# All of h by twenty block products for twenty-four, from the fifth unit on, in trees over six banks

## The chip, the cores and the metric

The kernel runs on one core of a Trainium2 chip, in f32 throughout. The metric is the device time of one execution in microseconds (us). The engines are PE (matmuls, with the weight loads PEld beside them), DVE, ACT, POOL, and SP, which issues most DMAs. Each engine runs its own queue of instructions in order; semaphores tie the queues together.

## The reference

```python
B, H, S, D = 4, 8, 768, 48
f = 1.0 / (1.0 + np.exp(-f_logit))
for t in range(S):
    state = f[:, :, t, :, None] * state + einsum('bhd,bhe->bhde', k[:, :, t], v[:, :, t])
    y[:, :, t] = einsum('bhd,bhde->bhe', q[:, :, t], state)
x = y.transpose(0, 2, 1, 3).reshape(3072, 384)
h = x @ w_in                                  # 384 x 2048
out = (h * (1.0 / (1.0 + np.exp(-1.702 * h)))) @ w_out     # 2048 x 384
```

A recurrence with a decay per channel (the attention part) makes x; a perceptron with the quick gelu follows.

## The kernel before, in words

**Units.** The 3072 tokens are cut into 12 units of 256 (4 batches of 3). Each has an attention part and a perceptron part. The attention of unit n + 1 is interleaved with the perceptron of unit n and earlier ones: `merge` (L1100) walks the attention's parts of a unit, and behind each takes as many items from a list `fill` of perceptron matmuls as its share of the columns says (`late`, L1141, gives the shares from unit 4 on; L1146 and the loop at L1178 the columns of a unit). PE's and POOL's queues hold the instructions in the order in which the program emits them; the queues of DVE and ACT are put in order by the tile framework's scheduler from unit 4's attention on (`fill_order.close()`).

**Attention.** Inputs come by DMA and are turned by DVE transpositions (`turn`, L338). In six levels, PE makes scores into the tile "sc" (two PSUM banks, one buffer: `score` L406), DVE and ACT evacuate them (`evacuate` L435, L445, L456), DVE multiplies the operands by products of the gates (`promote` L492), ACT sets copies aside (L463, L469), and v is shuffled on DVE (L304). POOL makes the products of the gates (L397, L365). In units 4 to 10, DVE turns k (L558), a DMA brings it to DRAM and back, and ACT copies it (`fetch_k`, L573). Then the part "S" (or "S1"): `add` (L503) begins the outputs in the tile "y" (two banks); PE makes the state increments into "sc" (L594); DVE updates the states (L612, L613); and the part "W" adds the states' share into "y" (L634), ACT copies it out (L646), DMAs bring it into xT, and POOL makes sums of its blocks (`sums_of_x`, eleven sums of 128 x 128, L856).

**Perceptron.** Units 0 to 2 run in blocks of four column tiles (`mlp_h` L980, `mlp_o` L994) while the weights are converted. Unit 3 makes h plainly (L980). From unit 3 on, the second matmul runs by seven products for eight (`mlp_o7`, L785), with sums of g on DVE (`sums_of_a`, L720 to L724, and `last_sum`, L729) and sums of w_out (T).

From unit 4 on ("the fifth unit on"), h is made by `mlp_h16` (L873): the first three quarters of the 2048 columns by sixteen block products for eighteen, the last quarter plainly. With w_in as blocks of 128 x 512 and xT as blocks of 128 x 128, `CHAINS` (L796) lists four chains of products `(weights, tokens, output)`, all of a chain accumulating in one bank; `SEQUENCE` (L804) gives the order and `LANE` (L805) the bank of each of four (tags mm0 to mm3). A product is four matmuls of 128 columns (L883). After some products of a chain, the bank's present sum is a share of an output block of h: ACT copies the first share into g (L897), DVE adds the second (L899) and ACT takes the gelu (L900); one output needs a gelu alone (L894). The last quarter's matmuls (L905, 256 columns, gelu L909) lie between. The last unit has one token more, so its products are of 129 columns and run in two groups of two matmuls.

The sums of weight blocks come from `sums_of_w` (L810: eleven sums, nine on POOL, L816, and two on DVE, L820), three behind each part of unit 4's attention as `chores`, and from `sums_in_place` (L829: seven sums that overwrite w_in, L840, L842), which unit 3's list holds behind its first eight matmuls of o (L1027), when plain h has been read for the last time.

Of the kernel before, what the change touches and what calls it, by code (L numbers as in the profile page):

```python
# [23 lines left out]
def kernel(  # L24
# [706 lines left out]
    def mlp_o7(n, g):  # L731
# [37 lines left out]
        def p3():  # L769
# [6 lines left out]
            ("Y", a(0, 0), b(0, 0), p1, True, 0), ("W", a(1, 1), T_(4), p4, True, 1),  # L776
# [18 lines left out]
    ROWS = NFF // FG - 1  # L795
    CHAINS = (  # L796
        (("D5", "b21", 3), ("N6", "E12", 2), ("C4", "E4", 4), ("N3", "E15", 0), ("a00", "E6", 1), ("N4", "E10", 5)),
        (("N5", "b21", None), ("N1", "b11", 1), ("D11", "E11", None), ("D8", "E3", 0)),
        (("a22", "E3", None), ("D9", "E9", 4), ("N7", "b10", None), ("N2", "E14", 2)),
        (("a10", "E0", None), ("D2", "b11", 3)),  # L800
    )
    NEGATIVE = 0, 2, 5

    SEQUENCE = "0 1 2 0 1 2 p 0 1 2 p 0 1 2 p 0 3 3 p 0".split()  # L804
    LANE = {"0": 0, "1": 1, "2": 2, "3": 1, "p": 3}  # L805
    lanes = {}
    WA = {f"a{i}{c}": w_in[:, c, i * FG * P:(i + 1) * FG * P] for i in range(ROWS) for c in range(NK)}
    assert ROWS == 3 and NK == 3

    def sums_of_w():  # L810

        for i in range(1, 8):
            WA[f"N{i}"] = const.tile([P, FG * P], F32, name=f"N{i}")

        def by(engine, op):
            return lambda out, x, y: lambda: engine.tensor_tensor(WA[out], WA[x], WA[y], op)  # L816
        plus, minus = by(nc.gpsimd, ALU.add), by(nc.gpsimd, ALU.subtract)

        def both_minus(out, x, y):
            return lambda: nc.vector.scalar_tensor_tensor(  # L820
                WA[out], WA[x], -1.0, WA[y], op0=ALU.mult, op1=ALU.subtract
            )
        yield from (
            both_minus("N4", "a00", "a20"), both_minus("N7", "a10", "a11"), plus("N6", "a20", "a21"),
            minus("N7", "N7", "N6"), plus("N2", "a12", "a22"), minus("N6", "N6", "N2"), plus("N6", "N6", "a10"),
            minus("N3", "a00", "a21"), plus("N1", "a01", "a21"), plus("N5", "a02", "a22"), plus("N5", "N5", "N4"),
        )

    def sums_in_place():  # L829

        assert not w_sums
        for new, old in (("D5", "a12"), ("D2", "a11"), ("D9", "a21"), ("C4", "a20"), ("D11", "a01"), ("D8", "a02")):
            WA[new] = WA[old]
        add, sub = ALU.add, ALU.subtract
        for engine, out, x, op, y in (
            (nc.gpsimd, "D5", "a12", sub, "a10"), (nc.vector, "D9", "a20", add, "a21"),
            (nc.vector, "C4", "a22", sub, "a20"), (nc.vector, "C4", "C4", add, "D5"),
            (nc.gpsimd, "D2", "a10", add, "a11"),
        ):
            engine.tensor_tensor(WA[out], WA[x], WA[y], op)  # L840
        for out, x, y in (("D11", "a01", "a00"), ("D8", "D11", "a02")):
            nc.vector.scalar_tensor_tensor(WA[out], WA[x], -1.0, WA[y], op0=ALU.mult, op1=ALU.subtract)  # L842

    def sums_of_x(n):
# [6 lines left out]

        def by(out, x, op, y):
            e.setdefault(out, None)
            if e[out] is None:
                e[out] = next(at)
            nc.gpsimd.tensor_tensor(e[out], e[x], e[y], op)  # L856

        add, sub = ALU.add, ALU.subtract
        by("E4", "b10", sub, "b00")
        by("E12", "E4", add, "b21")  # L860
        by("E3", "b20", add, "b21")
        by("E10", "b01", add, "b21")
        by("E0", "E10", sub, "b11")
        by("E15", "E12", add, "b11")
        by("E6", "E10", sub, "E15")
        by("E9", "b00", sub, "b21")
        by("E11", "b10", add, "b11")
        by("E11", "E11", add, "E3")
        by("E14", "E4", sub, "b20")

    E = {}

    def mlp_h16(n, g):  # L873
        w = (width(n) + 1) // 2
        banks, begun = {}, set()

        def product(group, chain, i, lane):
            a, b, out = CHAINS[chain][i]
            if i == 0:
                banks[chain] = bank([P, group.stop - group.start, w], f"h_{n}_{group.start}_{chain}", lane)  # L880
            ph = banks[chain]
            for t in range(group.start, group.stop):
                nc.tensor.matmul(  # L883
                    ph[:, t - group.start], lhsT=WA[a][:, t * P:(t + 1) * P], rhs=E[n][b],
                    start=(i == 0 and t == group.start), stop=(i == len(CHAINS[chain]) - 1), skip_group_check=True,
                )
            if out is None:
                return
            row, j = out // 2, out % 2
            f = row * FG + group.start  # L890
# [11 lines left out]
        def plain(f, lane):  # L902
            ph = bank([P, width(n)], f"h_{n}_p{f}", lane)
            for c in range(NK):
                nc.tensor.matmul(  # L905
                    ph, lhsT=w_in[:, c, (ROWS * FG + f) * P:(ROWS * FG + f + 1) * P], rhs=xTs[n][:, c, :], start=(c == 0),
                    stop=(c == NK - 1),
                )
# [302 lines left out]
```

## Time and profile before

| what | before |
|---|---|
| median of 3 runs (lowest, highest) | 616.76 us (615.52, 617.32) |
| profiled execution, its own time | 615.66 us |
| its span | 613.9 us |
| DVE, ACT, POOL busy | 66%, 44%, 20% |
| PE groups on the chain that ended last | h L883 19%, h L980 13%, h_p L905 7%, o_Y, o_Z, o_X and o_W L785 28% together |
| L492 on DVE (promote) | 45 of them, 1295 ns each |
| L899 on DVE (add of h) | 45, 627 ns |
| L897 and L900 on ACT (copy, gelu) | 45 each, 541 and 585 ns |
| L338 on DVE (transposition) | 36, 1108 ns |

The busy table says how much of the span each engine worked. The chain that ended last follows the end of the kernel back, at each step to what released it, and gives shares by engine and line. A timeline's row has the start, the duration, the engine, the line, the operation, what it writes and reads, and in brackets how long the engine stood still before it and what released it. Rows of PE group several matmuls, and neighbouring groups overlap, because matmuls are pipelined: what one costs PE is the distance of the starts.

### The profile page before, as it was taken

Reading aid. Unit: us, or ns where it says so; the run is one execution under the profiler, and the core shown is the slowest. Engines: PE = TensorE matmul, PEld = TensorE weight load, DVE = VectorE, ACT = ScalarE, POOL = GpSimd, SP = SyncE. Lnnn points to the kernel's source line nnn. Section 1 sums busy time; section 2 is a strip of 40 time slices with the busy share of each in tenths; the row PEclk is TensorE's granted clock in tenths of the full one; section 3 lists DMA queues with packets and bytes.
Section 4 is the critical chain, followed back from the end, with each engine's and each line's share of the span. In section 5 each row is a group of like instructions: output and inputs, shape, how many; then the busy total and the mean of one; then the engine's idle time right before and its main releaser. Section 6 shows DMA issues by size and latency. Waiting matters only on the chain.

```text
span 613.9 us, 18222 instructions
## 1 busy us (share of the span) xinstructions
PE 593.2 (97%) x7760; PEld 526.7 (86%) x7760; DVE 405.4 (66%) x649; ACT 271.5 (44%) x580; POOL 121.5 (20%) x201
## 2 busy tenths in 40 slices
PE   7969899969999999999999999999999999999997
PEld 5657676847677689999999999999999999999997
DVE  1788966665885856777667578667679565442254
ACT  3475633433333444454464364264364363343330
POOL 3020120020003802501401501501401402301100
PEclk9889999989999999999999999999999999999999
DMA  7756766553034453443453343453261121001000
GB/s 174 196 125 179 182 150 173 130 144 79 1 95 101 106 137 90 96 121 92 113 138 71 79 104 84 126 136 75 61 163 40 40 60 28 28 2 28 27 0 27
DMA packets 83313, 58.28 MB, mean 95 GB/s; under 512 B 33633, under 2 KB 75265, under 8 KB 83233
## 3 DMA queue, kind: packets, MB, share of 16 engines
q1 hardware_dynamic: 82480, 55.94, 36.6%
q10 hardware_dynamic: 753, 1.18, 0.8%
q8 instruction: 61, 1.00, 0.7%
q14 instruction: 19, 0.16, 0.1%
HBM read 43.98 MB, written 8.39 MB: 85 GB/s over the span
## 4 chain that ended last, share of the span: by engine, by line
PE 90%; DVE 5%; ACT 1%; DMA 1%; issue 1%; SPq 1%; DVEq 0%; ACTq 0%
PE h L883 19%; PE h L980 13%; PE o_Y L785 12%; PE o L994 9%; PE o_Z L785 8%; PE h_p L905 7%; PE sc L406 6%; PE o_X L785 4%; PE o_W L785 4%; PE t L350 2%; PE y L634 2%; PE y L503 2%; PE sc L594 2%; PE idle L114 1%; DVE a L227 1%
## 5 line engine op out<-in xcount | busy, mean ns | idle before, releaser
L492 DVE TENSOR_TENSOR X<-X,tot 128x1024 f32<-128x1024 f32 x45 | 58.3, 1295 | 56.2 <-PE sc L406 47.3
L980 PE MATMUL h<-xT,w_in 128*128 128x256 f32 x384 | 91.1, 393 | 0.1
L980 PEld LDWEIGHTS h<-xT,w_in 128*128 128x128 f32 x384 | 74.3, 197 | 12.7 <-DVE sum L1042 0.3
L463 ACT COPY Kc<-X 128x512 f32<-128x512 f32 x72 | 48.1, 668 | 77.3 <-DVE X L492 52.0
L994 PE MATMUL o<-w_out,g 128*128 128x384 f32 x192 | 65.9, 491 | 2.9 <-DVE w_out L228 2.9
L397 POOL TENSOR_TENSOR tot<-F 128x512 f32<-128x512 f32 x12 | 12.5, 1039 | 242.7 <-DVE st L612 236.4
L883 PE MATMUL h<-E,w_in 128*128 128x128 f32 (+1 forms) x448 | 58.0, 276 | 0.0
L994 PEld LDWEIGHTS o<-w_out,g 128*128 128x128 f32 x192 | 35.4, 190 | 25.2 <-DVE w_out L228 3.6
L883 PEld LDWEIGHTS h<-E,w_in 128*128 128x128 f32 x448 | 54.7, 192 | 1.2
L899 DVE TENSOR_TENSOR g<-g,h 128x512 f32<-128x512 f32 (+1 forms) x45 | 27.9, 627 | 39.1 <-PE h L883 38.8
L785 PE MATMUL o_Y<-T,S 128*128 128x192 f32 x288 | 51.6, 329 | 0.0
L785 PEld LDWEIGHTS o_Y<-T,S 128*128 128x128 f32 x288 | 47.1, 190 | 0.5
L984 ACT ACTIVATE g<-h 128x256 f32<-128x256 f32 x64 | 24.3, 385 | 52.0 <-PE h L980 51.4
L905 PE MATMUL h_p<-xT,w_in 128*128 128x256 f32 (+1 forms) x192 | 46.8, 380 | 0.0
L456 DVE COPY_PREDICATED A<-masks,sc 128x256 f32<-128x256 uint32 x96 | 42.2, 509 | 0.0
L897 ACT COPY g<-h 128x512 f32<-128x512 f32 (+1 forms) x45 | 23.7, 541 | 40.6 <-PE h L883 40.0
L338 DVE STREAM_TRANSPOSE X<-raw 128x512 f32<-128x512 f32 x36 | 38.0, 1108 | 3.3 <-PE y L634 3.0
L646 ACT COPY yT<-y 48x256 f32<-48x256 f32 x96 | 35.2, 366 | 8.5 <-PE y L634 7.3
L406 PEld LDWEIGHTS sc<-X,Kc 48*64 48x64 f32 x1440 | 27.1, 141 | 13.4 <-ACT Kc L463 7.4
L406 PE MATMUL sc<-X,Kc 48*64 48x64 f32 x1440 | 31.8, 228 | 6.5 <-DVE A L435 3.3
L905 PEld LDWEIGHTS h_p<-xT,w_in 128*128 128x128 f32 x192 | 34.0, 191 | 3.3
L900 ACT ACTIVATE g<-g 128x512 f32<-128x512 f32 (+1 forms) x45 | 25.9, 585 | 22.4 <-DVE g L899 22.4
(117 smaller groups left out, 1075.4 us busy)
## 6 DMA issues: line engine op xcount, KB each, us to landing
bits<-in_moe_w_out_dram SPq DMA_DIRECT2D x8, 768.0 KB, 7.1
raw<-in_f_logit_dram SPq DMA_DIRECT2D x48, 96.0 KB, 2.2
raw<-in_k_dram SPq DMA_DIRECT2D x48, 96.0 KB, 3.2
raw<-in_q_dram SPq DMA_DIRECT2D x44, 96.0 KB, 2.3
bits<-in_moe_w_in_dram SPq DMA_DIRECT2D x7, 576.0 KB
k_tok<-z SPq DMA_DIRECT2D x56, 64.0 KB, 1.7
kt<-k_tok SPq DMA_DIRECT2D x14, 256.0 KB, 2.8
xT<-yT SPq DMA_DIRECT2D x24, 144.0 KB, 2.6
```

The costliest lines, as they stand in the source:

```text
L338: nc.vector.transpose(view(out, at, [[HALF, NP], [step, R4], [R4 * step, 32]]), by_half[:, j, f].rearrange("p a (j d) -> p (a j) d", j=R4) ...
L406: nc.tensor.matmul(t["sc"][g * HS:(g + 1) * HS, h, a, s, :], lhsT=t["Kc", l][rows(h), x:x + HS], rhs=rhs(h, a, g), start=True, stop=True,)
L456: nc.vector.copy_predicated(out=view(A, at, dims), mask=mask.bitcast(U32), data=got)
L463: nc.scalar.copy(c.rearrange("p (n two m) -> p n two m", two=2, m=m), view(X, KF * SLOT, [[2 * m, SLOT // (2 * m)], [(KR - KF) * SLOT + m, ...
L492: nc.vector.tensor_tensor(x, x, y, ALU.mult)
L646: nc.scalar.copy(view(yT[rows(h)], at, [[U, NP], [step, HS]]), py[columns(h, g), g, :, f, :])
L785: nc.tensor.matmul(t[name], lhsT=lhs(f), rhs=rhs(f), start=(new and i == 0), stop=(i == HF - 1), skip_group_check=True,)
L883: nc.tensor.matmul(ph[:, t - group.start], lhsT=WA[a][:, t * P:(t + 1) * P], rhs=E[n][b], start=(i == 0 and t == group.start), stop=(i == ...
L899: nc.vector.tensor_tensor(to, to, ph, ALU.add)
L905: nc.tensor.matmul(ph, lhsT=w_in[:, c, (ROWS * FG + f) * P:(ROWS * FG + f + 1) * P], rhs=xTs[n][:, c, :], start=(c == 0), stop=(c == NK - 1),)
L980: nc.tensor.matmul(ph, lhsT=w_in[:, c, ff * P:(ff + 1) * P], rhs=xTs[n][:, c, :], start=(c == 0), stop=(c == NK - 1))
L994: nc.tensor.matmul(t["po"], lhsT=g[ff // FG][:, ff % FG, tt * P:(tt + 1) * P], rhs=w_out[:, ff, :], start=(ff == ffs[0]), stop=(ff == ffs[ ...
```

## The change

`mlp_h20` takes the place of `mlp_h16`: all four quarters of h, 24 block products, are made by 20 products. `PRODUCTS` lists them as `(weights, tokens, parent, parts)`. A product without a parent begins a bank; one with a parent goes on in its parent's bank, or in a copy of it, which ACT makes from bank to bank (three in a unit of 128 columns). `parts` says to which outputs the bank's sum is added after the product, and with which sign. `WHOLE` gives the order and the bank ("lane") of each product: lanes 0 to 3 are mm0 to mm3, lanes 4 and 5 the two banks of the tile "y". `HALVES` does so for the last unit, forty products of two matmuls, where lanes 6 and 7, the banks of "sc", are used too. Per unit DVE now adds ten times (before five; one of the ten has both operands in SBUF), ACT copies seven first shares (five) and three banks, and takes eight gelus on 512 columns (six, and four on 256).

The sums change with it: `sums_of_w` has fourteen (nine POOL, five DVE, with some of DVE's reading POOL's), `sums_in_place` nine (four POOL, five DVE), `sums_of_x` twelve. In `mlp_o7` the product W takes its terms in the plain order. As "y" and "sc" are banks of h now, `merge` emits all that is left of earlier units' h ahead of a part "S" or "S1".

```diff
-            ("Y", a(0, 0), b(0, 0), p1, True, 0), ("W", a(1, 1), T_(4), p4, True, 1),
+            ("Y", a(0, 0), b(0, 0), p1, True, 0), ("W", a(1, 1), T_(4), p4, True, 0),
...
+    PRODUCTS = (
+        ("c1", "q0", -1, ((0, -1),)), ("p1", "v", 2, ((6, -1),)), ("a21", "w", -1, ((5, -1),)), ("p3", "r3", 4, ((0, -1),)),
+        ("p4", "q4", 13, ((6, 1),)), ("p5", "b11", 13, ((7, 1),)), ("p6", "b20", 1, ((4, 1),)), ("p7", "s7", -1, ((3, 1),)),
+        ("c4", "w", 9, ((2, 1), (0, -1))), ("p9", "x", 7, ((1, -1),)), ("a20", "q0", 19, ((4, -1),)),
+        ("p11", "y", 3, ((1, -1),)), ("p12", "b00", 10, ((2, 1),)), ("a30", "t", 18, ()), ("p14", "b01", 17, ((3, 1),)),
+        ("p15", "b10", 0, ((6, 1),)), ("p16", "u", 6, ((5, 1),)), ("c2", "t", 18, ()), ("c3", "s7", -1, ()),
+        ("p19", "z", 17, ((5, -1),)),
     )
...
+    WHOLE = tuple((x, 0, lane) for x, lane in (
+        (18, 0), (0, 2), (7, 1), (2, 3), (17, 4), (15, 2), (9, 1), (13, 0), (19, 5), (1, 3),
+        (14, 4), (4, 2), (10, 5), (6, 3), (8, 1), (3, 2), (5, 0), (16, 3), (12, 5), (11, 2),
+    ))
...
+        for engine, out, x, op, y in (
+            (pool, "c1", "a01", "+", "a02"), (ve, "p4", "c1", "-", "a30"), (pool, "p15", "a21", "+", "a31"),
+            (pool, "c2", "a11", "+", "a12"), (ve, "c3", "a30", "", "a32"), (pool, "c4", "a02", "", "a00"),
+            (ve, "p6", "c2", "+", "a22"), (pool, "p15", "p15", "", "p4"), (pool, "p12", "a11", "", "c4"),
+            (ve, "p6", "p6", "", "c3"), (pool, "p16", "a20", "", "a21"), (pool, "p12", "p12", "+", "a10"),
+            (ve, "p16", "p16", "", "a22"), (pool, "p12", "p12", "+", "a20"),
+        ):
...
+        for engine, out, at, x, op, y in (
+            (pool, "k", "a02", "a02", "+", "a30"), (ve, "p7", "a01", "a11", "", "c3"), (ve, "p19", "a12", "c2", "-", "a20"),
+            (pool, "p3", "a02", "a11", "", "k"), (ve, "p5", "a31", "a31", "", "c3"), (pool, "p1", "a32", "a21", "+", "c3"),
+            (ve, "p9", "a11", "c4", "", "a11"), (ve, "p11", "a00", "a00", "", "c1"), (pool, "p14", "a10", "a10", "", "c2"),
         ):
...
+        def take(lane, name):
+            if lane < 4:
+                banks[lane] = bank([P, wide, w], f"h_{n}_{name}", lanes["h"][lane])
+            else:
+                tag = "y" if lane < 6 else "sc"
+                if tag not in shared:
+                    shared[tag] = ps.tile([P, 2, 512], F32, tag=tag, name=f"h_{n}_{tag}")
+                banks[lane] = shared[tag][:, lane % 2, :wide * w].rearrange("p (t x) -> p t x", x=w)
+            return banks[lane]
+
+        def product(x, group, lane):
+            a, b, parent, parts = PRODUCTS[x]
+            root = parent < 0
+            ph = take(lane, f"{x}_{group}") if root else banks[lane]
+            kids = [y for y in range(len(PRODUCTS)) if PRODUCTS[y][2] == x]
+            goes_on = any(lane_of[y, group] == lane for y in kids)
+            for t in range(wide):
+                f = group * wide + t
                 nc.tensor.matmul(
+                    ph[:, t], lhsT=WA[a][:, f * P:(f + 1) * P], rhs=E[n][b], start=(root and t == 0), stop=not goes_on,
+                    skip_group_check=True,
                 )
+            in_y[n] -= 1
+            for y in kids:
+                if lane_of[y, group] != lane:
+                    nc.scalar.copy(take(lane_of[y, group], f"{y}_{group}"), ph)
+            part, turned = ph, 1
+            for out, sign in parts:
...
+                if key in single:
+                    nc.scalar.activation(to, ph, AF.Gelu_apprx_sigmoid, scale=float(sign))
+                    continue
+                if key not in begun:
+                    begun.add(key)
+                    nc.scalar.activation(to, ph, AF.Copy, scale=float(sign))
+
+                    part, turned = to, sign
+                    continue
+                nc.vector.tensor_tensor(to, to, part, ALU.add if sign == turned else ALU.subtract)
+                if not left[key]:
+                    nc.scalar.activation(to, to, AF.Gelu_apprx_sigmoid)
...
+            while kind in ("S", "S1") and any(in_y.get(m) for m in range(n)):
+                w, emit, _ = fill.pop(0)
+                emit()
+                done += w
...
-    H16 = 16 * FG * G + FG * NK * U
+    H20 = 20 * FG * G
```

A product is named below by its weights and tokens' index in the list: c3 (18) begins a bank, c2 (17) goes on in a copy of it in "y", p19 (19) in a copy of c2's, a20 (10) and p12 (12) on that; p14 (14) goes on in c2's bank; p4 (4) and p5 (5) go on behind a30 (13), p3 (3) and p11 (11) behind p4; p6 (6) and p16 (16) behind p1 (1).

## The prediction

> **What bounds the kernel now.** I read the busy table first, then the chain that ended last, then the timeline of PE through one unit, then the queues of DVE, ACT and POOL beside it.
>
> ```profile
> span 613.9 us, 18222 instructions
> ...
> PE 593.2 (97%) x7760; PEld 526.7 (86%) x7760; DVE 405.4 (66%) x649; ACT 271.5 (44%) x580; POOL 121.5 (20%) x201
> ...
> PE 90%; DVE 5%; ACT 1%; DMA 1%; issue 1%; SPq 1%; DVEq 0%; ACTq 0%
> ```
>
> PE is the bound. Stretches of one unit (44.6 us) from 260 us on show PE busy without a hole, so any product saved is time saved, and any new wait of PE is time lost in full: there is no slack on PE to hide it. The timeline of PE in unit 7 gives the prices (columns: start, duration of the group; groups overlap, so starts are subtracted):
>
> ```profile
> 393.80 1.05 PE L883 MATMUL h<-xT,w_in 128*128 128x128 f32 x8
> 394.69 1.06 PE L883 MATMUL h<-xT,N 128*128 128x128 f32 x8
> ...
> 400.45 1.46 PE L905 MATMUL h_p<-xT,w_in 128*128 128x256 f32 x6
> 401.75 1.95 PE L883 MATMUL h<-E,w_in 128*128 128x128 f32 x16
> ```
>
> A product (4 matmuls, 8 records) takes 394.69 - 393.80 = 0.89, so 0.223 a matmul; three plain matmuls of 256 columns take 401.75 - 400.45 = 1.30, so 0.433 each.
>
> **1. Work saved.** Before, a unit's h is 64 x 0.223 + 12 x 0.433 = 14.29 + 5.20 = 19.49; after, 80 x 0.223 = 17.86. That is 1.63 less in each of units 4 to 11: **-13.0**. Nothing else leaves PE.
>
> **2. First seam: the sums of w (near 208 us).** DVE's sums are chores of unit 4's attention. These are the rows:
>
> ```profile
> 194.94 2.06 DVE L338 STREAM_TRANSPOSE F<-raw 128x512 f32<-128x512 f32 x2 [0.83 <-DMA vt<-in_v_dram]
> 199.96 1.14 DVE L338 STREAM_TRANSPOSE X<-raw 128x512 f32<-128x512 f32 x1 [2.96 <-PE y L634]
> ...
> 206.66 0.73 DVE L456 COPY_PREDICATED A<-masks,sc 128x256 f32<-128x256 uint32 x1
> ```
>
> ```profile
> 197.01 1.28 POOL L816 TENSOR_TENSOR N<-w_in 128x512 f32<-128x512 f32 x1
> ...
> 204.62 1.04 POOL L365 TENSOR_SCALAR F<-F 128x1024 f32<-128x1024 f32 x1
> ```
>
> Between the first two DVE rows the changed kernel's order has four sums, and three of them wait for POOL. The last is p16, whose POOL half is POOL's seventh sum after 197.0, with the L365 among them: 197.05 + 7 x 1.28 + 1.04 = 207.05, and DVE's own half (0.69) ends at 207.75. Behind it in DVE's queue stand the transposition of 199.96 and the evacuations, up to the row at 206.66: shifted by 7.8. PE's scores L406 follow, which start at 208.50 before, right behind 18 matmuls of L994 that began at 202.60. There DVE had 1.1 in hand, and without POOL beside it its chain takes 6.5 instead of 7.4; so the scores start at about 214.35, **+5.9**. Nothing covers it: PE's order is written out, and its next instruction is this one. Bounds: 4.4 with 1.04 for a sum (as L397's rows of that size), 7.5 with 1.47 (the fourth sum's row).
>
> **3. The clock.** What a stand costs behind itself is seen at the start:
>
> ```profile
> 42.24 1.13 PE L406 MATMUL sc<-X,Kc 48*64 48x64 f32 x32 [3.33 <-DVE A L435]
> ```
>
> From 40 to 47 us the granted clock was 0.60, where it is 1.00 from 34 to 40. That is 2.8 us of full clock lost, of which some 1.1 fell in the stand, so 1.7 behind it. Another stand of 1.9 us at 131.6 has 0.50 from 134 to 136 behind it, 1.0 lost. I take **+1.2** for seam 2 (0 to 3.4, twice the first). The Trainium skill ("TensorE: Matmul & The Clock Gate", Part 1: The HAM clock gate) says that an idle window of about 3.4 us halves the clock, and that a busy one gives it back; it speaks against any edit that makes PE stand longer than that. By the page alone the price would be half of one window, 1.7 (an estimate), as in the first of the two rows.
>
> **4. Second seam: sums in place (near 254 us).** POOL's reductions end at 244.2 and two in-place sums (L840, 2.51) come before xT's sums; DVE's first sum there runs at 245.48, its evacuation ends at 252.90, the scores start at 253.98. After, DVE's p9 stands behind three POOL sums (3 x 1.28, to 248.0), a shift of 1.9, so the evacuation ends at 254.8 where PE, earlier by its saved work, would ask at 253.65: **+1.4** with 0.2 lag (0 to 2.2).
>
> **5. Banks in units 4 to 9.** Before, DVE adds 5 times in a unit and no bank is waited for in steady units. After, it adds ten times, ACT copies 3 banks, and each bank is taken again soon. I walked the three queues in the changed kernel's order: 0.20 from a PE row's end to its consumer, add 0.69 (0.60 apart), copy 0.59, gelu 0.63, transposition 1.11 (L338, L558), promotion L492 1.25, kn copy L573 1.15. The same walk of the kernel before gives 44.6 a unit without a wait, as the trace has. In unit 7, from the start of h:
> - The 11th product (p14) waits 0.14: its bank and p19's are one tile "y", so in the built program it waits for p19's add, though that reads the other bank.
> - a20, in the second bank of "y", waits likewise for p14's add, which stands behind a transposition (L558) and ends at 12.89; a20 could start at 12.2: 0.71.
> - a20's copy stands behind ACT's kn copy, so p6's add runs only at 15.84, a promotion (1.25) follows, p3's add ends at 19.56, and the last product p11, which goes on in that bank, waits for it: 0.39.
> - the last gelus push the second kn copy to 22.49, and the state scores L594 wait for it: 0.73.
>
> Sum 1.97, more than the 1.63 saved. By the same walk the waits are 2.9, 3.0, 1.5, 2.0, 1.4 and 1.5 in units 4 to 9 (in 4 and 5 a shuffle, L304, stands between the adds too, so p11 waits 0.8 and 1.4 and L594 1.4): **+12.3**. These are some 24 waits; 0.2 more or less in each (the lag itself) makes it 7.5 to 17.1.
>
> **6. Unit 10.** Its remaining h must now be emitted before the state part of unit 11's attention, as the banks of "y" are taken. Before, h lay between the state scores and the outputs that need the states:
>
> ```profile
> 545.34 1.10 PE L594 MATMUL sc<-vt,kn 64*64 64x48 f32 x64
> 546.37 2.05 PE L883 MATMUL h<-E,w_in 128*128 128x128 f32 x16
> ...
> 552.41 1.11 PE L634 MATMUL y<-X,st 48*48 48x64 f32 x64
> ```
>
> That is 6 us of cover. After, only three L785 (1 us) lie there, and DVE's chain of state updates (L612, L613: 7 x 0.39 = 2.7, behind sums S of the unit) is waited for in four steps of 1.3, 0.3, 0.7 and 0.4; with 0.2 at "y", **+3.0** (1.5 if DVE gets to the chain at once, 4 if two more sums lie ahead).
>
> **7. Unit 11.** Here a product is 2 matmuls of 129 columns, 0.447. A bank's copy or add (0.38 to 0.42, as the rows on 258 columns) with 0.2 lag is longer than that, so a bank may be taken again only two products later; nine times in 40 products PE comes too early, by 0.18 to 1.25, in all 4.7. One wait of before goes:
>
> ```profile
> 581.49 0.71 PE L883 MATMUL h<-xT,w_in 128*128 128x129 f32 x4 [0.48 <-ACT g L894]
> 582.04 0.61 PE L883 MATMUL h<-xT,N 128*128 128x129 f32 x4
> ```
>
> (582.04 - 581.49 = 0.55 instead of 0.45: a restart costs 0.1 more, which all waits above hold.) That is 0.7 with the time before it, so **+4.0** (2.2 to 5.8).
>
> **Hidden.** The twelfth sum of xT on POOL (0.45, L856's row) lies in POOL's idle 80%; if it were late, the first product would wait 0.1 to 0.5 (the walk has 0.14 in the unit it starts in). That W of the o products takes its terms in the other order costs PE nothing: same matmuls.
>
> **Sum**, against the profiled execution, 615.66 (its span 613.9; it is 1.1 under the median of the runs, 616.76, so the sum may read 1 low): 615.66 - 13.0 + 5.9 + 1.2 + 1.4 + 12.3 + 3.0 + 4.0 = **630.5**.
>
> **The rivals.**
> - *The sums are in time.* If the two seams cost nothing (2, 3 and 4 fall, 8.5), 622. For it: POOL is 20% busy. Against: DVE runs its queue in order, and the sums that it waits for are POOL's seventh in a row. 0.10, with 619 to 624.
> - *The seams are worse.* The slowest sum of before took 2.15 (POOL beside DVE's promotions); with 1.47 to 2.15 and the clock's upper bound, 638 to 641. 0.12.
> - *Faster.* The waits for banks in items 5 and 7 aren't there, since consumers come sooner than my walk has them: 615.66 - 13.0 + 8.5 + 3.0 - 0.7 = 613.5. This decides where those waits come to less than 4 us in all, under 0.5 a unit. For it: DVE is idle a third of the time and ACT over half. Against: it isn't their load but their order, a 1.1 transposition or copy ahead of a 0.6 add. 0.15, of which 0.03 within 0.3%.
> - *It doesn't save what it says*, since loading the weights bounds a narrow matmul. Spoken against: 0.223 for 128 columns beside 0.433 / 2 = 0.217 in the wide ones. Under 0.01, and in the forecast's share.
>
> **How the numbers follow.** The forecast with its bounds (624 to 638) has 0.63. The range takes in the first rival at the low end and half of the second at the high end: 619 to 639. A measurement of this kernel can tell about 0.3% (1.9 us) from no change: faster 0.12, within it 0.03, slower 0.85.
>
> **What would show it.** PE idle for 5 to 6 us before L406 near 208, released by DVE's evacuation, and a slice of the clock below 9 there; short waits of the products, released by DVE's adds and ACT's copies, in every unit; L594 released by the kn copy; L634 in unit 11's attention released by the state updates; a unit's stretch of 44.1 to 46 instead of 44.6. Wrong it would be if units took 43 (no waits), or if DVE passed 208 in time.

## The result, and the profile after

The changed kernel took 643.29 us (median of 4 runs, 641.68 to 643.94), the kernel before 616.14: a ratio of 1.045 with a 95% interval of 1.040 to 1.050. Run again later, the same kernel took 639.34 (6 runs, 636.71 to 645.36) beside 614.92, a ratio of 1.041 (1.037 to 1.045). So the change loses 24 to 27 us, where 14.8 were forecast (630.5 us, with a range of 619 to 639): the direction was right, the size was not.

The busy table, the clock by slices and the chain that ended last, from the page of the changed kernel:

```profile
span 642.2 us, 18494 instructions
...
PE 594.6 (93%) x7824; PEld 527.2 (82%) x7824; DVE 435.8 (68%) x697; ACT 291.7 (45%) x611; POOL 128.2 (20%) x211
...
PEclk9989899979999699999999999999999999998999
...
PE 64%; DVE 17%; ACT 8%; issue 4%; DMA 2%; SPq 2%; POOL 1%; DVEq 0%; ACTq 0%; POOLq 0%
```

PE's share of the chain fell from 90% to 64%; DVE's rose from 5% to 17%, ACT's from 1% to 8%. PE's busy time did not fall by 13 us, it rose by 1.4. That is no sign that the products cost more: a matmul at half clock counts as twice as long (the same ten rows of L785 take 3.36 us in this profile, at half clock from 576.41 on, and 1.73 in the later one, at full clock), and the mean granted clock is 0.971 for 0.986 before. (A kernel below, e9, with the same products and a clock of 0.991, has 578.9, 14.3 less than before.)

The largest stands of PE after, from its timeline (in brackets: how long PE stood, and what ended it):

```profile
205.01 5.97 PE L996 MATMUL o<-w_out,g 128*128 128x384 f32 x18
218.94 1.14 PE L406 MATMUL sc<-Qc,Kc 48*64 48x64 f32 x32 [7.96 <-ACT Kc L463]
...
269.59 0.69 PE L406 MATMUL sc<-Qc,Kc 48*64 48x64 f32 x32 [3.44 <-DVE A L456]
```

The 7.96 is put down to ACT's copy L463, which ended at 218.19 + 0.62 = 218.81 and had itself waited for DVE's promotion L492:

```profile
218.19 0.62 ACT L463 COPY Kc<-X 128x512 f32<-128x512 f32 x1 [1.34 <-DVE X L492]
```

DVE's evacuation ended at almost the same time (below, 218.08 + 0.71 = 218.79). Either way PE waits for DVE's queue. The group of scores behind it takes 1.14 where the same group took 0.69 before: half clock.

**Where it went, stage by stage.** The unit's state scores L594 mark the stages (units are counted from 0, as in the kernel; the expectation of e5 below calls the marks of units 3 and 4 those of units 4 and 5). In the second profile of the changed kernel (span 634.9) against before (613.9), from mark to mark:

| stretch | before | after | difference | forecast |
|---|---|---|---|---|
| start to unit 3's L594 | 190.23 | 188.69 | -1.5 | 0 |
| to unit 4's (first seam) | 47.01 | 56.65 | +9.6 | +7.1 |
| to unit 5's (second seam, h of unit 4) | 44.59 | 51.41 | +6.8 | +2.7 |
| next five (h of units 5 to 9) | 222.91 | 225.02 | +2.1 | +1.3 |
| rest (h of units 10 and 11) | 109.16 | 113.13 | +4.0 | +3.7 |

In the first profile of the changed kernel the same stretches are 192.63, 57.04, 51.44, 225.05 and 116.0: the two executions differ by 3.9 us ahead of the change's first edit and by 2.9 behind unit 10, for which see the clock.

The first seam on DVE, and on POOL, in the timelines of the changed kernel:

```profile
197.34 2.06 DVE L338 STREAM_TRANSPOSE F<-raw 128x512 f32<-128x512 f32 x2 [0.83 <-POOL tot L397]
200.73 1.74 DVE L838 SCALAR_TENSOR_TENSOR N_p<-N_c,w_in 128x512 f32<-128x512 f32 x1 [1.33 <-POOL N_c L840]
203.64 1.75 DVE L840 TENSOR_TENSOR N_p<-N_c,w_in 128x512 f32<-128x512 f32 x1 [1.17 <-POOL N_c L840]
205.42 1.41 DVE L840 TENSOR_TENSOR N_p<-N_p,N_c 128x512 f32<-128x512 f32 x1
210.43 1.73 DVE L840 TENSOR_TENSOR N_p<-N_p,w_in 128x512 f32<-128x512 f32 x1 [3.60 <-POOL N_p L840]
212.09 1.07 DVE L338 STREAM_TRANSPOSE X<-raw 128x512 f32<-128x512 f32 x1
...
218.08 0.71 DVE L456 COPY_PREDICATED A<-masks,sc 128x256 f32<-128x256 uint32 x1
```

```profile
199.42 1.28 POOL L840 TENSOR_TENSOR N_c<-w_in 128x512 f32<-128x512 f32 x1
...
204.81 1.48 POOL L365 TENSOR_SCALAR F<-F 128x1024 f32<-128x1024 f32 x1
206.26 1.69 POOL L840 TENSOR_TENSOR N_p<-N_p,N_p 128x512 f32<-128x512 f32 x1
```

DVE waits for POOL three times, as forecast, but a sum on DVE takes 1.74 beside a sum on POOL, not 0.69, and POOL's seven with L365 end at 210.39, 10.97 after their start, not 10.0. The transposition of X starts 14.75 after F's, where before it was 5.02: a shift of 9.7, not 7.8.

### The profile page after: what moved, and what is told of

It is laid out like the page before. It is cut to its first block, busy times and chain, and to the rows that moved or that the text cites. A ratio compares the mean times of both kernels' runs of the same rounds, so it can differ in the third digit from the quotient of the medians.

```text
span 642.2 us, 18494 instructions
## 1 busy us (share of the span) xinstructions
PE 594.6 (93%) x7824; PEld 527.2 (82%) x7824; DVE 435.8 (68%) x697; ACT 291.7 (45%) x611; POOL 128.2 (20%) x211
## 4 chain that ended last, share of the span: by engine, by line
PE 64%; DVE 17%; ACT 8%; issue 4%; DMA 2%; SPq 2%; POOL 1%; DVEq 0%; ACTq 0%; POOLq 0%
PE h L982 11%; PE h L905 9%; PE o_Y L785 9%; PE o L996 8%; PE o_Z L785 6%; PE sc L406 6%; DVE g L928 4%; PE h_y L905 3%; PE o_W L785 3%; PE o_X L785 3%; PE t L350 2%; DVE X L492 2%; ACT kn L573 2%; ACT g L930 2%; ACT yT L646 1%
## 5 line engine op out<-in xcount | busy, mean ns | idle before, releaser
L492 DVE TENSOR_TENSOR X<-X,tot 128x1024 f32<-128x1024 f32 x45 | 57.7, 1283 | 48.0 <-PE sc L406 40.5
L463 ACT COPY Kc<-X 128x512 f32<-128x512 f32 x72 | 48.1, 668 | 92.4 <-DVE X L492 68.5
L996 PE MATMUL o<-w_out,g 128*128 128x384 f32 x192 | 68.7, 508 | 2.9 <-DVE w_out L228 2.9
L996 PEld LDWEIGHTS o<-w_out,g 128*128 128x128 f32 x192 | 36.9, 198 | 26.7 <-DVE w_out L228 3.6
L905 PE MATMUL h<-E,w_in 128*128 128x128 f32 (+1 forms) x428 | 55.0, 276 | 2.5 <-DVE g L928 2.5
L905 PEld LDWEIGHTS h<-E,w_in 128*128 128x128 f32 x428 | 51.1, 192 | 3.2 <-issue 3.2
L785 PE MATMUL o_Y<-T,S 128*128 128x192 f32 x288 | 52.3, 336 | 0.0
L930 ACT ACTIVATE g<-g 128x512 f32<-128x512 f32 (+1 forms) x63 | 35.6, 582 | 32.0 <-DVE g L928 31.8
L785 PEld LDWEIGHTS o_Y<-T,S 128*128 128x128 f32 x288 | 48.6, 195 | 0.5
L986 ACT ACTIVATE g<-h 128x256 f32<-128x256 f32 x64 | 24.0, 382 | 54.4 <-PE h L982 53.8
L646 ACT COPY yT<-y 48x256 f32<-48x256 f32 x96 | 35.1, 366 | 12.2 <-PE y L634 11.1
L928 DVE TENSOR_TENSOR g<-g,h 128x512 f32<-128x512 f32 (+1 forms) x49 | 31.3, 645 | 10.6 <-PE h L905 5.0
L338 DVE STREAM_TRANSPOSE X<-raw 128x512 f32<-128x512 f32 x36 | 38.0, 1106 | 0.1
L924 ACT ACTIVATE g<-h 128x512 f32<-128x512 f32 (+1 forms) x52 | 28.2, 554 | 15.4 <-PE h L905 14.4
L365 POOL TENSOR_SCALAR F<-F 128x1024 f32<-128x1024 f32 x11 | 13.1, 1193 | 106.3 <-ACT F L368 83.5
L928 DVE TENSOR_TENSOR g<-g,h_y 128x512 f32<-128x512 f32 (+1 forms) x26 | 16.4, 632 | 25.0 <-PE h_y L905 25.0
```

Source lines behind the costliest of these rows:

```text
L338: nc.vector.transpose(view(out, at, [[HALF, NP], [step, R4], [R4 * step, 32]]), by_half[:, j, f].rearrange("p a (j d) -> p (a j) d", j=R4) ...
L463: nc.scalar.copy(c.rearrange("p (n two m) -> p n two m", two=2, m=m), view(X, KF * SLOT, [[2 * m, SLOT // (2 * m)], [(KR - KF) * SLOT + m, ...
L492: nc.vector.tensor_tensor(x, x, y, ALU.mult)
L646: nc.scalar.copy(view(yT[rows(h)], at, [[U, NP], [step, HS]]), py[columns(h, g), g, :, f, :])
L785: nc.tensor.matmul(t[name], lhsT=lhs(f), rhs=rhs(f), start=(new and i == 0), stop=(i == HF - 1), skip_group_check=True,)
L905: nc.tensor.matmul(ph[:, t], lhsT=WA[a][:, f * P:(f + 1) * P], rhs=E[n][b], start=(root and t == 0), stop=not goes_on, skip_group_check=True,)
```

## The experiments

All are the changed kernel with one or more edits, but for the last two: e11 has no edit, and e12 is the kernel before with one. The measured price of an edit is read from its stretch where it can be, since whole executions of one kernel spread over 5 to 9 us (before 613.06 to 618.09, the change 636.71 to 645.36).

### Sums of w all on POOL (e1_w_pool)

```diff
-        ve, pool = nc.vector, nc.gpsimd
+        ve = pool = nc.gpsimd
```

(in `sums_of_w`; POOL makes p4 by a product with -1 and a difference.)

> Every sum of w (first seam) is made by POOL; DVE has none between its transpositions. Theory (DVE's queue stood behind POOL's sums): PE's wait of 7.96 us at 218.9 goes, and with it about 2 us at a lower clock behind it, so 643.3 - 10 = 633 us, ratio to before 1.028. Rival (POOL's work itself slows DVE's chain, whoever makes the sums): POOL has more sums now, a wait of 4 us or more stays there, 638 us or more.

Measured: 627.83, ratio to before 1.022 (1.016 to 1.027). There is no stand at the first seam, and the stretch is 47.01, as before the change. So the seam is 9.6 to 10.0 us, all of it DVE's queue behind POOL; the rival falls. POOL's fifteen sums slowed some promotions (L492 1.5 to 2.2 beside them, for 1.23), which was hidden here. The other 5 us of the whole are the differences of executions described above.

### p9 on POOL (e2_p9_pool)

```diff
-            (ve, "p9", "a11", "c4", "", "a11"),
+            (pool, "p9", "a11", "c4", "", "a11"),
```

> Of the sums in place (second seam) only p9 moves from DVE to POOL. Theory (DVE stands behind three POOL sums for p9): the wait of 3.44 us at 269.6 goes, with some 1.8 us of clock behind it: 643.3 - 5 = 638 us. Rival (the end of the chain is late because last_sum and promote run slower beside POOL): at most 1.5 us less, 642 us.

Measured: 637.82, ratio 1.039 (1.033 to 1.044). The stand of 3.44 became 1.37, with full clock behind it; the stretch fell from 51.4 to 47.6. Both theories had a part: the wait for POOL's sums was 2.1 with 1.7 of clock, and 1.4 stay, since POOL's sums run beside last_sum and the promotions. (The median of the whole can't decide between them: it is 5.5 us under the first result of the change and 1.5 under the repeated one.) DVE in that seam:

```profile
256.18 2.30 DVE L492 TENSOR_TENSOR X<-X,tot 128x1024 f32<-128x1024 f32 x1
258.40 0.70 DVE L435 TENSOR_TENSOR A<-sc,masks 128x512 f32<-128x512 f32 x1
259.00 1.17 DVE L729 TENSOR_TENSOR g<-g,S 128x512 f32<-128x512 f32 x1
260.10 2.28 DVE L492 TENSOR_TENSOR X<-X,tot 128x1024 f32<-128x1024 f32 x1
```

The promotion with two operands in SBUF takes 2.3 for 1.23; L435, which reads PSUM, takes its usual 0.70.

### Without DVE's additions (e3_no_adds)

```diff
-                nc.vector.tensor_tensor(to, to, part, ALU.add if sign == turned else ALU.subtract)
```

> All of DVE's additions to outputs of h (L928) are left out, so each output block has its first share alone; products, copies and gelus stay. Theory (the products do save 1.63 us a unit, and DVE's adds hold the banks): no wait of a product for DVE, state scores no longer late behind the gelus, units 5 to 9 at 43.0 us, last unit's h 18 to 19 us; about 18 us less, 625 us. Rival (twenty narrow products with copies cost more PE time than counted, or ACT's copies hold the banks): units stay at 44 us or more and the whole above 635.

Measured: 618.75, ratio 1.007 (1.005 to 1.009). Units 5 to 9 take 42.97 each, no product waits:

```profile
336.61 0.57 PE L594 MATMUL sc<-vt,kn 64*64 64x48 f32 x28
```

```profile
379.58 1.10 PE L594 MATMUL sc<-vt,kn 64*64 64x48 f32 x64
```

379.58 - 336.61 = 42.97, 1.61 less than 44.58. So the 1.63 a unit of saved work is real, and DVE's additions are what eats it. This run doesn't tell whether by their work or by their place in the queues; the orders below (e7, e9) show that part of it is their place. The two seams are still in this kernel (stands of 7.95 and 3.48).

### Two tiles for y (e4_split_y)

```diff
-                tag = "y" if lane < 6 else "sc"
+                tag = f"y{lane - 4}" if lane < 6 else "sc"
```

(and `add`, L634 and L646 take the tile of their g.)

> The tile y is two tiles of one bank each, so that a product in one bank no longer waits for a reader of the other. My walk of the queues: p14 and a20 wait less, but the adds that come later still hold p11 and the state scores: 1.5 us less in all, 642 us. Rival (the shared tile is what makes most of the waits of units 4 to 10): 5 us less or more, 638 us.

Measured: 641.75, ratio 1.043 (1.039 to 1.048). The stretches of units 5 to 9 sum to 225.4, as without the edit: the waits for the other bank went, and p11 and the state scores waited as much longer (1.24 and 1.08 in unit 7). Neither gain came. The shared tile alone costs nothing.

### PE kept busy in the first seam (e5_keep_busy)

```diff
+            if (n, count_sc[n]) == AT:
+                pt = ps.tile([P, 2, 512], F32, tag="y", name="busy")
+                for _ in range(13):
+                    nc.tensor.matmul(pt[:, 0, :320], lhsT=ident, rhs=masks.rearrange("p l f t -> p (l f t)"), start=True, stop=True)
```

(in `scores`; AT is the second tile of scores of unit 4's attention.)

> Thirteen matmuls of 320 columns that nobody reads (some 7.0 us of PE) fill the stand of 7.96 us in the first seam, ahead of the scores that wait there; nothing else is changed. Theory (a stand makes the clock fall behind itself): the stand is still paid in full, but the scores and matmuls behind it run at full clock, 0.5 us a group of scores for 1.0, and the stretch from unit 4's state scores to unit 5's is 55.0 us for 57.0; 641 us in all. Rival (the clock falls there for another reason, or by chance): the stretch stays at 57 us, 643 us.

Measured: 634.87, ratio 1.032 (1.027 to 1.037); the stretch is 55.09 for 56.65 and 57.04. PE in this kernel:

```profile
206.31 7.16 PE L432 MATMUL busy<-masks,ident 128*128 128x320 f32 x26
214.48 0.69 PE L407 MATMUL sc<-Qc,Kc 48*64 48x64 f32 x32 [1.01 <-ACT Kc L469]
```

Here the same scores run at 0.69 and the granted clock is 1.00 from 214.4 to 221.4. So the lower clock comes from the stand, and not from the place; the theory holds. (The rest of the gain in the whole is the early part, and a different order of DVE in units 4 and 5, whose waits are shorter here.)

### Cover in unit 10 (e6_cover)

```diff
+            if kind == "S" and n == NALL - 1:
+                n_columns = max(n_columns, 16 * HC)
             some(first + n_columns)
```

> In the last attention part, 16 matmuls of o (5.2 us, from the same list) are put between the state scores and the outputs that need the states, where the change leaves three. Theory (unit 10's missing cover): the waits of 1.10, 0.47 and 0.22 us with their restarts go, 2.7 us by my walk, and with them up to 3.4 us of lower clock behind them; 637 to 641 us. Rival (the state updates are late because of DVE's own queue, whatever PE has): the waits move to the next instructions and the time stays at 643 us.

Measured: 636.04, ratio 1.034 (1.029 to 1.039). The last stretch of the table takes 110.5 for 113.1, 2.6 less, against 2.7 by the walk. Without the edit, PE stands twice for a state update:

```profile
573.24 1.10 PE L634 MATMUL y<-X,st 48*48 48x64 f32 x36 [1.10 <-DVE st L613]
574.81 1.09 PE L634 MATMUL y<-X,st 48*48 48x64 f32 x28 [0.47 <-DVE st L613]
```

With it, no stand is left there. The waits did not move on.

### Other orders (e7_orders), and all remedies with two more (e8_all)

e7 has new `WHOLE` and `HALVES` and the two tiles of y:

```diff
-        (18, 0), (0, 2), (7, 1), (2, 3), (17, 4), (15, 2), (9, 1), (13, 0), (19, 5), (1, 3),
-        (14, 4), (4, 2), (10, 5), (6, 3), (8, 1), (3, 2), (5, 0), (16, 3), (12, 5), (11, 2),
+        (18, 2), (2, 1), (7, 4), (17, 5), (1, 1), (13, 2), (9, 4), (14, 5), (19, 0), (4, 3),
+        (6, 1), (0, 5), (10, 0), (3, 3), (8, 4), (15, 5), (12, 0), (16, 1), (11, 3), (5, 2),
```

> The same twenty products in other orders and banks, found by searching for orders in which a bank is taken again late: whole units so that consumers may be over 1 us late, the last unit's halves so that none waits; the tile y is two tiles. Seams and unit 10 are as in the change. Theory (the order over the six banks makes the waits, not their number): my walk gives 9.1 us less, 634 us. Rival (any order waits, since DVE's and ACT's queues hold other work ahead of the adds): at least 639 us.

What these two kernels compute isn't the reference's h. A likely reason, which no run takes by itself, is that a copy of a bank goes into a bank that matmuls of o had written on 192 columns only. Number, kind and size of the instructions are the same, so the times can be compared. Measured: 629.18, ratio 1.022 (1.018 to 1.027). In its profile the waits of products are gone but one (0.39); the stretches of h from unit 5 on give 4.6 less, unit 4's 1.8, so 6.4 of the 9.1 us of the walk. The state scores still wait about 1 us for kn's copy behind the last gelus in three units. So most of the bank waits were made by the order, as the theory has it, and part of them moved on.

e8 adds the remedies of e1, e2 and e6, and

```diff
-            nc.scalar.copy(t["kn"][:, :, f, :], z.rearrange("p d a -> p a d"))
+            nc.gpsimd.tensor_copy(t["kn"][:, :, f, :], z.rearrange("p d a -> p a d"))
...
-            while kind in ("S", "S1") and any(in_y.get(m) for m in range(n)):
+            while kind in ("S", "S1") and any(in_y.get(m) or m in in_y and in_o.get(m, 0) < 4 for m in range(n)):
```

> All remedies together: sums of w on POOL, p9 on POOL, cover in unit 10, y as two tiles, the new orders, part S1 only behind four matmuls of o, kn's copy on POOL instead of ACT. Theory (the 13.0 us of saved products are there and were spent on waits): 643.3 - 15.5 - 5.5 (as measured for the first two) - 14 (my walk for the rest) = 608 us, faster than before (614.3). Rival (POOL's added copies and sums slow DVE, or the products themselves cost more than counted): above 615 us.

Measured: 627.27, ratio 1.019 (1.015 to 1.023): my theory fell by 19 us. PE stands 6.05 at 248.5, and 1.3 to 2.4 before a group of scores in each unit. The first is seen on DVE and POOL, whose sums came later here and ran through DVE's sums of g:

```profile
240.40 1.52 DVE L842 TENSOR_TENSOR w_in<-w_in,N_c 128x512 f32<-128x512 f32 x1
241.84 1.75 DVE L724 TENSOR_TENSOR S<-g 128x512 f32<-128x512 f32 x1
243.52 1.75 DVE L842 TENSOR_TENSOR w_in<-w_in,N_c 128x512 f32<-128x512 f32 x1
245.19 2.28 DVE L492 TENSOR_TENSOR X<-X,F 128x1024 f32<-128x1024 f32 x1
```

```profile
248.50 2.93 PE L788 MATMUL o_X<-w_out,g 128*128 128x192 f32 x8 [6.05 <-ACT o_X L751]
```

ACT's copy of a bank for o stood behind its copy aside, this behind DVE's promotion, and that behind sums at two and a half times their price. Part S1, put later, left less matmul work between it and the next scores.

### Remedies without these two (e9_all_b), and without the orders (e10_seams)

e9 is e1, e2, e6 and two tiles for y, with kn on ACT and S1 in its old place, and with this order on the banks that the change has (and an order of `HALVES` without waits):

```diff
+        (18, 0), (2, 3), (0, 2), (7, 1), (17, 4), (1, 3), (15, 2), (13, 0), (19, 5), (9, 1),
+        (6, 3), (4, 2), (10, 5), (14, 4), (5, 0), (3, 2), (12, 5), (8, 1), (16, 3), (11, 2),
```

> Sums of w on POOL, p9 on POOL, cover in unit 10, the tile y as two tiles, whole units in another order on the same banks (found by a search that asks for late consumers and for the banks of y to be free at the end), last unit in an order without waits. kn's copies stay on ACT and part S1 where it was. Theory (the saved 13.0 us are there; seams, orders and one missing cover ate them): 643.3 - 15.5 - 5.5 (as measured) - 13.6 (walk) = 609 us, 608 to 613 with what builds differ by, faster than before (614.4). Rival (waits move on to the state scores and evacuations): above 616 us.

Measured: 611.73 (12 runs), ratio to before 0.9955 (0.9934 to 0.9976): faster than both kernels, by 3 us and by 28 to 32. The last unit's h takes 18.5 us, 20.26 before and 22.99 in the change. Not all of the 3 us need be the products' work: in the profiles, 1.6 us of the difference lie from unit 3's L594 on (422.0 for 423.6), and the rest lies ahead of every edit, where executions differ anyway. So most of the 13 is still lost, above all to waits for evacuations:

```profile
341.59 0.69 PE L406 MATMUL sc<-Qc,Kc 48*64 48x64 f32 x32 [1.02 <-DVE A L456]
...
386.14 0.69 PE L406 MATMUL sc<-Qc,Kc 48*64 48x64 f32 x32 [1.51 <-DVE A L456]
...
474.97 0.69 PE L406 MATMUL sc<-Qc,Kc 48*64 48x64 f32 x32 [1.54 <-DVE A L456]
```

e10 has e1, e2 and e6 alone.

> Sums of w on POOL, p9 on POOL and cover in unit 10, but the orders, banks and tiles of the change. Theory (seams and cover are half of the loss, orders the other half): 643.3 - 15.5 - 5.5 - 2.7 = 620 us, 617 to 622. Rival (the first two overlap, since what each took out was in part the difference between builds ahead of the seams): 624 us or more.

Measured: 620.30, ratio 1.009 (1.006 to 1.011), as the theory had it. From 639.3 (the change beside it) to 620.3 by seams and cover, to 611.7 by order and tiles (the last unit's h alone goes from 22.99 in the change to 18.5).

### The changed kernel again (e11_again)

No edit.

> The changed kernel once more, unchanged, beside the others. If the part ahead of the first seam (188 to 193 us up to the same state scores in kernels with the same instructions there) differs by execution, its profile may now show 188 to 190 us there and its median 639 to 642 us; if it differs by program, 192 to 193 us and 643 us again. From the seam on it should repeat its waits of 7.96 and 3.44 us.

Measured: 639.34, with 188.69 us up to the first seam and stands of 7.95 and 3.48. So the part ahead of the seam differs by execution (192.63 in the first), and the stands repeat.

### Stands of chosen length (e12_stands)

The kernel before, with chains of 1 to 9 additions on DVE between two matmuls, twice in each of units 5 to 10:

```diff
+        nc.tensor.matmul(pt[:, 0, :P], lhsT=ident, rhs=probe[:, :P], start=True, stop=True)
+        nc.vector.tensor_copy(probe[:, :P], pt[:, 0, :P])
+        for _ in range(k):
+            nc.vector.tensor_tensor(probe, probe, probe, ALU.add)
+        nc.tensor.matmul(pt[:, 1, :P], lhsT=ident, rhs=probe[:, :P], start=True, stop=True)
```

> The kernel before with twelve stands of PE put into units 5 to 10: a matmul, a chain of 1 to 9 additions on DVE, and a matmul that reads its end, so PE waits 1.5 to 9 us each time. Theory of the prediction (a stand costs some 1.2 us of clock behind it only if it is long, some 3.4 us): full clock behind the short ones, a lower one behind those of 4 us and more. Rival (a stand of 1 to 2 us lowers the clock too, depending on where it falls): lower clock behind some short ones, by 1 to 3.5 us. The sum of the waits is added to the time, some 50 us, 665 us.

Measured: 698.1 in one execution, 83 us more than before and not 50. The stands came to 54.4 us and the clock behind them (table below) to 22.1, which the 665 left out; the other 7 or so were not traced. The rows of three of the twelve:

```profile
327.47 0.49 PE L1151 MATMUL stand<-probe,ident 128*128 128x128 f32 x2 [1.87 <-DVE probe L1150]
...
518.65 0.79 PE L1151 MATMUL stand<-probe,ident 128*128 128x128 f32 x2 [2.69 <-DVE probe L1150]
...
566.69 0.80 PE L1151 MATMUL stand<-probe,ident 128*128 128x128 f32 x2 [9.93 <-DVE probe L1150]
```

Windows behind the first two of these (the length, then PE's busy time; PEclk, the granted clock, is the third number from the end):

```profile
327.50:330.90 3.40, 3.40 (x25) 3.25 (x26) 1.57 (x3) 0.38 (x1) 0.00 (x0) 1.00 0.74 184
...
518.70:522.10 3.40, 3.40 (x16) 3.40 (x17) 0.00 (x0) 0.00 (x0) 0.00 (x0) 0.50 0.00 0
```

The full clock lost behind each stand, from one-microsecond windows over the 11 us behind it (sum of 1 less PEclk):

| stand, us | 1.5 | 1.9 | 2.7 | 2.8 | 3.3 | 3.4 | 4.1 | 4.2 | 5.6 | 7.2 | 7.8 | 9.9 |
|---|---|---|---|---|---|---|---|---|---|---|---|---|
| lost, us | 0 | 0 | 3.1 | 1.7 | 1.7 | 2.9 | 1.7 | 1.7 | 1.7 | 2.5 | 2.1 | 3.0 |

Stands of 2.7 and more lost 1.7 to 3.1 us each time here, whatever their length. Elsewhere, one of 1.92 lost 1.7 in the kernel before and 3.4 in the first profile of the change (at 134 us), ones of 2.4 in e8 lost 3.2, 1.7 and nothing, one of 2.94 in the kernel before (at 128 us) lost nothing, and ones up to 1.5 alone lost nothing. So the rival was nearer: the limit isn't near 4 us, and the length of a stand doesn't tell by itself.

What does tell is in the clock records of the traces. In all fourteen, the granted clock is full or half, and it changes only at times that are whole multiples of 3.41 us apart; where these times lie differs from execution to execution. The stretch between two neighbouring such times is called a slot here. Half clock lasts one slot or several, and a slot of it costs 1.71 us, or less where part of it falls into the stand. The kernel before, cut at these times:

```profile
123.37:126.78 3.41, 1.78 (x7) 0.84 (x5) 3.24 (x7) 1.19 (x2) 1.81 (x2) 1.00 0.79 142
126.78:130.19 3.41, 2.11 (x7) 1.31 (x8) 3.31 (x4) 0.00 (x0) 2.37 (x5) 1.00 0.70 211
130.19:133.61 3.42, 1.50 (x12) 0.62 (x14) 1.85 (x3) 1.53 (x3) 0.00 (x0) 1.00 0.73 198
133.61:137.02 3.41, 3.41 (x128) 3.31 (x128) 0.76 (x2) 2.05 (x5) 0.00 (x0) 0.50 0.24 57
```

The stand of 2.94 us ends at 128.08. It is cut into 1.63 and 1.30, and the clock stays full. The shorter one, of 1.92, lies whole in the third slot, and the fourth is at half clock. (In e6 that stand lies whole in one slot too, and the clock stays full.) In e12 the same stand of 2.94 us falls otherwise, 2.24 of it into one slot, and is paid for:

```profile
122.03:125.44 3.41, 1.17 (x4) 0.38 (x2) 3.29 (x5) 1.10 (x2) 2.34 (x3) 1.00 0.58 113
125.44:128.85 3.41, 2.71 (x4) 1.50 (x5) 3.14 (x4) 0.08 (x1) 1.84 (x4) 0.50 0.80 224
```

Over the fourteen traces, slots at full clock in which PE was busy for under 40% were followed by half clock in 30 of 30 cases, those with 40 to 60% in 25 of 47, those with more in 4 of 2276. So it counts how much of a stand falls into one slot, and for stands of 2 to 4 us that is luck of the execution. The Trainium skill ("TensorE: Matmul & The Clock Gate", Part 1: The HAM clock gate) has an idle window of about 3.4 us as the condition. The slots here have that length, but stands of 2.69 and 2.77, which are shorter, were paid for, as was the one of 1.92 in the kernel before. The measurement decides.

## Why the prediction was right and wrong, point by point

The forecast was 630.5 us, the results 643.3 and 639.3. The terms for the saved work, the banks and units 10 and 11 came within 1.1 us each. Three terms were too small: the first seam by 2.1 us, the second by 2.0, and the clock by 2.3 to 6.1.

**1. Work saved: right.** 1.61 a unit (e3), 1.63 forecast.

**2. First seam: right in mechanism, short in size.** A stand of 7.96 for 5.9, above the step's upper bound (7.5; by the terms that it names, the bounds come to 4.2 and 7.2, not 4.4 and 7.5). The term that failed is "DVE's own half (0.69)" and the 1.28 a POOL sum: beside each other they took 1.74 and up to 1.69. The profile of before had the row that tells it: in the second seam an addition of 128 x 512 on DVE ran beside POOL's and took 1.75, where the next one, with POOL idle, took 0.68:

```profile
245.48 1.75 DVE L840 TENSOR_TENSOR w_in<-w_in 128x512 f32<-128x512 f32 x1 [1.32 <-POOL w_in L840]
247.16 0.68 DVE L729 TENSOR_TENSOR g<-g,S 128x512 f32<-128x512 f32 x1
```

I used the price of an addition that reads PSUM (L899).

**3. Clock: the step that failed most.** I counted 1.2 once. Behind the first seam 2.2 were lost in the first profile (1.8 in the second), behind the second seam 1.7 in both, and in the first profile 3.4 behind unit 10's short stands, which in the second cost none: 7.3 us in the first profile and 3.5 in the second. The step had read its own two rows too short. In the kernel before, half clock goes on from 41.45 to 48.28 us (the granted clock from 47.00 to 48.30 is 0.51), so 3.0 us were lost behind the stand of 3.33 and not 1.7; behind the stand of 1.92 it goes on from 133.61 to 137.02, 1.7 us and not 1.0. And the step counted one stand: behind the second seam, where item 4 had a stand of 1.4, it put the clock at nothing. The first profile behind unit 10, by slots of the clock (see e12), and then the second:

```profile
571.40:574.81 3.41, 1.72 (x42) 1.13 (x40) 3.20 (x9) 0.00 (x0) 0.00 (x0) 1.00 0.00 0
574.81:578.22 3.41, 3.41 (x50) 3.40 (x51) 0.69 (x2) 2.15 (x6) 0.00 (x0) 0.50 0.02 5
```

```profile
566.69:570.10 3.41, 2.03 (x42) 1.44 (x41) 3.24 (x8) 0.00 (x0) 0.00 (x0) 1.00 0.00 0
570.10:573.52 3.42, 2.89 (x55) 2.76 (x56) 0.96 (x3) 2.28 (x7) 0.00 (x0) 1.00 0.02 5
```

In the first, the stands of 1.10 and 0.47 lie within one slot; in the second, a slot ends inside the shorter one. The upper bound of the step, 3.4 in all, was too low: each stand is paid anew, and in e8 4.8 us were lost behind the one of 6.05.

**4. Second seam: right in mechanism, 3.44 for 1.4.** The three POOL sums took 3.90, as worked out (3.84). The shift that I put down, 1.9, doesn't follow from the step's own rows: 248.0 less 245.48 is 2.5, and 2.6 was measured by the release alone. Besides, last_sum behind p9 ran beside POOL too and took 1.75 for 0.68 before (p9's 1.74 is no more than the sum in its place took before):

```profile
260.73 1.74 DVE L840 TENSOR_TENSOR w_in<-N_c,w_in 128x512 f32<-128x512 f32 x1 [3.90 <-POOL w_in L840]
262.40 1.75 DVE L729 TENSOR_TENSOR g<-g,S 128x512 f32<-128x512 f32 x1
```

Seams and their clock together came to 14.8 (9.6 + 3.5 + 1.7) in the second profile, 8.5 in the forecast: that is 6.3 of the 7.7 us by which the forecast of the change's own effect was short (22.5 us in the table without its first row, 14.8 forecast). Of the first result another 5.7 us are differences of executions: 2.4 ahead of the first seam, where a stand of 1.9 at 134 us lost 3.4 of clock for 1.7 in before's profile, 2.9 behind unit 10, and 0.4 at the first seam.

**5. Banks in units 4 to 9: right.** 13.4 for 12.3: units 5 to 9 are 3.1, 1.1, 2.7, 1.1 and 2.1 above e3's 42.97 (forecast 3.0, 1.5, 2.0, 1.4, 1.5), unit 4 some 3.3 (2.9; its stretch of 51.4 less 42.97, the seam's 3.5 and its clock 1.7). The three waits of unit 7 stand where the walk put them:

```profile
427.22 1.16 PE L905 MATMUL h_y<-E,w_in 128*128 128x128 f32 x8 [0.39 <-DVE g L928]
...
434.10 1.13 PE L905 MATMUL h<-E,w_in 128*128 128x128 f32 x8 [0.36 <-DVE g L928]
...
436.91 1.15 PE L594 MATMUL sc<-vt,kn 64*64 64x48 f32 x64 [0.31 <-ACT kn L573]
```

The bracket counts from the modelled end of the matmul before. By the starts, a20 is 0.56 late (427.22 less 425.77 + 0.89), p11 0.53 (434.10 less 432.68 + 0.89), L594 0.5, for 0.71, 0.39 and 0.73. Most of the rest of the unit's 2.7 is a wait of scores for an evacuation (0.59 in brackets, 0.76 by the starts), which the list left out. That the sum over the units comes so near is in part luck, since single units are 0.7 over to 0.4 under.

**6 and 7. Units 10 and 11: right.** About 2.9 for 3.0, and 4.4 for 4.0 (h of the last unit 22.99 for 20.26, and 1.63 of work saved).

**The rivals.** Sums in time: no. Worse seams: it came nearest in value (638 to 641), and with the right cause (POOL beside DVE), but the price rose on DVE more than on POOL. Faster: not in this order; e9 shows that the same products can be, by 3 us in the medians and by 1.6 from the first edit on in the profiles.

## What to carry to other kernels

When work is saved on the engine that bounds, the price of the change is the order it puts on the engines beside it: walk their queues with rows that ran in the same company, not with the cheapest row of the same shape. A stand of the matmul engine costs its length and, where some 2 us or more of it fall into one slot of the clock (3.41 us), mostly 1.7 to 3.4 us more, each time anew. And a bank order can be made by search: asking that every bank be taken again late, and those that others need be free at the end, took 8.6 us off here (620.3 to 611.7, with y as two tiles), with the same products, and in whole units on the same banks.

## What the runs showed of the hardware

- DVE instructions with two operands in SBUF slow down while POOL works: an addition of 128 x 512 from 0.69 to as much as 1.75, a promotion L492 from 1.23 to as much as 2.3. Those that read PSUM (L435, 0.70) and transpositions (L338, two in 2.06) keep their time in the same company. The Trainium skill ("GPSIMD Engine Reference", 1. Specifications) says that the two share their SBUF interfaces and names DVE instructions with two SBUF inputs among those that contend; the rows agree, and give the price, a factor of up to 1.9 for the promotion and 2.5 for the addition.
- Half clock comes in slots of 3.41 us, whose places are fixed within an execution and differ between executions (all fourteen traces). So behind a stand it has a price that doesn't grow with the length: 1.70, one slot, in half of the long stands, up to 3.1 in the others (e12).
- In the built program, a tile of two banks is waited for as one (p14 and a20 in the change), but taking that wait away alone gave nothing (e4).
